# Gate and up of an FNet + GEGLU kernel: the last two contraction tiles taken into the seven Strassen products, and the columns run through in two passes with prepared weights fetched back

## The chip, the cores and the metric

One core of a Trainium2 chip runs the whole program. The metric is the device time of one execution in microseconds (us). Three executions of the kernel before took 781.22 (the median), 781.18 and 783.29 us. The engines are PE (matrix multiply; PEld is its weight load, which runs beside it), DVE (vector), ACT (scalar), POOL (GpSimd) and SP (here it only issues DMAs). Each engine takes its instructions in program order, and waits where one of them waits.

## The reference

```python
xn = _layernorm(x)                                     # x: 2048 x 448
a, b = xn @ dft_hid_re.T, xn @ dft_hid_im.T
s = dft_seq_re @ a - dft_seq_im @ b                    # 2048 x 2048 by 2048 x 448, twice
h = gelu_tanh(xn @ w_gate) * (xn @ w_up)               # 448 -> 1792
g = silu(h @ w_down)                                   # 1792 -> 448
out = x + s * g
```

Everything is float32. The kernel gets float32 accuracy out of PE by splitting each operand into a high part (a rounded copy, made by ACT) and a low part (the rest, a subtraction on DVE), and by multiplying high by high, high by low and low by high: three matmuls for one product.

## The kernel before

The 2048 rows lie in four chunks of 512 columns of the transposed activation (`xth[c]`, `xtl[c]`, high and low), and the 448 features lie in four contraction tiles of 128: tiles 0 to 2 are full, tile 3 has 64 features, with their low parts stacked under them, so that tile 3 needs two matmuls in place of three. The 1792 hidden columns are 14 blocks `f` of 128.

Four stages follow each other on PE. (1) Normalizing, transposing and plain gate and up products for blocks 0 and 1, up to 72 us. (2) Blocks 2 to 13, from 72 to 408 us, in 24 steps: a step is one block `f` with one pair `p` of chunks (2p and 2p+1), written in `strassen`, L372. (3) The transform along the hidden axis, `hid_mm`, to 489.5 us. (4) The transform along the sequence, to the end.

A step of stage 2 does gate and up of two chunks. Contraction tiles 0 and 1 go through Strassen's seven products with Winograd's sums: seven calls of `three` (L357) into four PSUM banks x1 to x4 (x1, x3 and x4 are used twice). Tiles 2 and 3 are added in plain products by `other` (L364), five matmuls for each of the four outputs; one of these, up of the second chunk, has a bank of its own, x5. A step has 41 matmuls of 512 columns. Between them stand up to four calls `dn[0]` to `dn[3]`, each of which takes one entry of the list `dq`: a down product of an earlier block pair, six matmuls of 448 columns (`down_one`), whose result DVE adds to `gacc` (L349). DVE takes the sums of the seven products from PSUM, ACT applies gelu, and the hidden values are split into high and low (`hs`). The last part of that for the second chunk is put off into the next step (`late`).

The sums of activations that Strassen needs, `t1` to `t4` of each pair (`combine`, L179), are made once, before and in the first steps. The sums of weights are made by `prep_s` (L238) for each block: four additions on POOL, copies on ACT, subtractions on DVE. Blocks go two at a time (`GROUPS`), and each block meets both pairs before the next two come: (0, f), (0, f+1), (1, f), (1, f+1), as (pair, block). So in each step either one block of weights or one pair of down weights (`prep_d`) is prepared, at the call `preps` in the middle of the step, and weights lie in three slots of `a_w`.

Beside this, stage 2 makes the sums of the sequence matrices that stage 4 needs (`sum_step`, L646): in every third step SP copies two halves of 896 KB from one DRAM tensor to another, and two steps later POOL issues two DMAs that add a second tensor to them. SP's DMAs land in the order of issue; POOL's run on a queue of their own.

Of the kernel before, what the change touches and what calls it, by code (L numbers as in the profile page):

```python
# [47 lines left out]
def fnet_geglu(ctx: ExitStack, tc: tile.TileContext, x, ca, ct, cp, et, wgu, wd, out):  # L48
# [29 lines left out]
    a_w = [a_ws[:, 2560 * i :][:, :2560] for i in (0, 2, 1)]  # L78
# [18 lines left out]
    th, tl = [None, None], [None, None]  # L97
# [71 lines left out]
    def turn_split(*turned):  # L169
        for c, k, pt in turned:  # L170
            nc.scalar.activation(xth[c][:, :, k * P : (k + 1) * P], pt, AF.Copy)
        for c, k, pt in turned:
            nc.scalar.activation(xf[c][:, :, k * P : (k + 1) * P], pt[:, :2], AF.Copy)
        for c, k, pt in turned:
            sl = slice(k * P, (k + 1) * P)
            nc.vector.tensor_sub(xtl[c][:, :, sl], pt, xth[c][:, :, sl])


    xf = [part(a_t, 1024 * (c + 1), 2, 512) for c in range(2)] + [None, None]  # L179

    def combine(p):


        (b11, b21), (b12, b22) = [[xf[c][:, k] for k in range(2)] for c in (2 * p, 2 * p + 1)]
# [4 lines left out]
        t = sb.tile([P, 2, 4, 512], FR, name=f"thl{p}", tag=f"u{p}")  # L189
        th[p], tl[p] = t[:, 0], t[:, 1]  # L190
        t = b11, b22, b12, b21

        def one(i):
            split(th[p][:, i], tl[p][:, i], t[i])

        return one


    loads = [0]

    def raw_tile():
        loads[0] += 1
        return a_r[:, 1536 * (loads[0] % 2) :][:, :1536]

    def load_w(f):
        raw = raw_tile()
        nc.sync.dma_start(raw[:, :1024], wgu[f].rearrange("p b f -> p (b f)"))
        return raw
# [34 lines left out]
    def prep_s(slot, raw, eng):  # L243


        w = a_w[slot]
        a21, a11, a12, a22 = [raw[:, i * P : (i + 1) * P] for i in range(2, 6)]
        s1, s2, s3, s4 = [raw[:, i * P : (i + 1) * P] for i in range(8, 12)]
        eng.tensor_add(s1, a21, a22)
        eng.tensor_sub(s3, a11, a21)  # L250
        eng.tensor_sub(s2, s1, a11)
        eng.tensor_sub(s4, a12, s2)
        nc.scalar.activation(w[:, :256], raw[:, :256], AF.Copy)
        nc.scalar.activation(w[:, 256:1408], raw[:, 384:], AF.Copy)
        nc.vector.tensor_sub(w[64:, :256], raw[64:, :256], w[64:, :256].bitcast(F32))
        nc.vector.tensor_sub(w[:, 1408:], raw[:, 384:], w[:, 256:1408].bitcast(F32))

        names = ("k3g", "k3u", "a11", "a12", "a22", "k2g", "k2u", "s1", "s2", "s3", "s4")
        parts = {}
        for i, n in enumerate(names):  # L260
            h = w[:, i * P : (i + 1) * P]
            l = w[:, 1408 + (i - 2) * P : 1408 + (i - 1) * P] if i >= 2 else None
            parts[n] = h, l
        return parts

    def load_d(grp):
        rv = raw_tile()[:, : 2 * D].rearrange("p (f d) -> p f d", f=2)
# [4 lines left out]

    def prep_d(grp, rv, late=False):
        w = a_d[grp[0] // 2 % 2].rearrange("p (a f d) -> p a f d", a=2, f=2)
# [89 lines left out]
    def other(ps, w, g, c, first=False):  # L364

        three(ps, w["k2" + "gu"[g]], (xth[c][:, 2], xtl[c][:, 2]), first)
        for xt in (xth[c], xtl[c]):
            nc.tensor.matmul(  # L368
                ps, w["k3" + "gu"[g]][0], xt[:, 3], start=False, stop=True, skip_group_check=True
            )  # L370

    def strassen(f, p, w, late, dn, preps):  # L372
# [5 lines left out]
        t1, t2, t3, t4 = [(th[p][:, i], tl[p][:, i]) for i in range(4)]  # L378
# [3 lines left out]

        x1 = bank(1)
# [9 lines left out]
        three(x3, w["s3"], t3, True)  # L393
        nc.vector.tensor_add(m, u, x3)
        x4 = bank(4)
        three(x4, w["s1"], t1, True)
        nc.vector.tensor_add(m, m, x4)
        three(x1, w["a12"], b21)
        other(x1, w, 0, c)
# [11 lines left out]
        other(x3, w, 1, c)  # L411
# [10 lines left out]
        other(x4, w, 0, e)  # L422
# [17 lines left out]
    with tc.manual_schedule():  # L440
# [109 lines left out]
        s_raw = load_w(GROUPS[1][0])  # L550
# [28 lines left out]
        xf[2] = part(a_t, 0, 2, 512)  # L579
# [18 lines left out]
        norm(1)  # L598

        nws = [None, None]  # L600


        for c in (2, 3):
            if c == 2:
                draw = load_d(GROUPS[1])
            else:
                s_raw2 = load_w(GROUPS[1][1])
            m0, h0, l0 = gateup(0, c, ws[0])
            between, between1 = [lambda: (m0(), h0()), l0], []
            if c == 2:  # L610

                xf[3] = part(a_g[1], 2560, 2, 512)
# [8 lines left out]
            else:  # L621
                between = [
                    lambda: (m0(), h0(), late_split(0)),
                    lambda: (l0(), late_split(1)),
                    lambda: late_split(2),
                    lambda: late_split(3),
                ]
            down(0, c - 1, wdn, between)
            if c == 2:
                nws[0] = prep_s(2, s_raw, nc.vector)  # L630
            else:
                nwdn, low_d = prep_d(GROUPS[1], draw, late=True)
                late_split = combine(1)
            m1, h1, l1 = gateup(1, c, ws[1], between1)
            m1()
            if c == 2:
                h1()
                l1()
                late_split = combine(0)
# [22 lines left out]

        dq = [(0, 3, wdn, kk) for kk in range(4)]
# [5 lines left out]
        nop = lambda: None  # L669

        slots = [2, 0, 1]
        e_at = {}
        for gi in range(1, len(GROUPS)):
            grp = GROUPS[gi]
            nxt = GROUPS[gi + 1] if gi + 1 < len(GROUPS) else None
            ws, wdn = nws, nwdn
            nws, n_raw = [None, None], {}

            def low_then_load():
                low_d()  # L680
                n_raw[0] = load_w(nxt[0])

            def prep_first():
                if gi == 1:
                    ws[1] = prep_s(slots[1], s_raw2, nc.vector)

            def prep_a():
                if gi == 1:
                    for n in range(4):
                        late_split(n)  # L690
                elif nxt:
                    nws[0] = prep_s(slots[2], n_raw[0], nc.gpsimd)
                else:
                    e_split(0)

            def prep_d_next():
                nonlocal nwdn
                if gi == 1:
                    nws[0] = prep_s(slots[2], n_raw[0], nc.gpsimd)
                    n_raw[1] = load_w(nxt[1])  # L700
                if nxt:
                    nwdn = prep_d(nxt, n_raw["d"])
                else:
                    e_split(1)
# [500 lines left out]
```

## Time and profile before

| what | us |
|---|---|
| median of three executions | 781.22 |
| profiled execution, whole | 780.67 |
| profiled execution, span from the first to the last instruction | 778.9 |
| stage 1, to the first product of `strassen` | 72.0 |
| stage 2, 24 steps | 336.5 |
| stage 3 | 81.1 |
| stage 4 | 289.4 |
| POOL's tensor instructions in stage 2, per 128 columns, alone | 0.46 |

Read the page from the engine that is busiest: its share of the span, then the chain that ended last, then what the other engines wait for. The mean duration of one matmul in the groups is longer than the distance between two, since matmuls overlap; the chain gives the distance.

### The profile page before, as it was taken

To read this page: it belongs to the slowest core of one execution; us is meant where nothing else is said; L and a number is where in the kernel's file an instruction comes from. 1 tells how busy PE (TensorE), PEld (TensorE's weight loads), DVE (VectorE), ACT (ScalarE), POOL (GpSimd) and SP (SyncE) were. 2 spreads that over 40 slices of the span, in tenths; PEclk is the share of its full clock that TensorE was granted. 3 is DMA by queue.
4 is the path that set the end of the run, shared out by engine and by line. 5 is a ranking of instruction groups with operands and counts; after the bars stand their busy time and mean duration, and the time that the engine had idled before them with its cause. 6 is when DMAs were issued, how large, how long until landed. Compare 5 with 4: busy or idle time off the path is not lost.

```text
span 778.9 us, 11227 instructions
## 1 busy us (share of the span) xinstructions
PE 772.5 (99%) x4092; PEld 695.8 (89%) x4092; DVE 594.5 (76%) x1052; ACT 310.5 (40%) x436; POOL 52.7 (7%) x83
## 2 busy tenths in 40 slices
PE   9999999999999999999999999999999999999997
PEld 8988888888888888888889999999999999999997
DVE  7877877767766776776675676888797887979797
ACT  3774432331332222322232855544444444444441
POOL 2000211110110010100000000000000000000000
PEclk9999999999999999999999999999999999999999
DMA  8000575353292360547000651688797969697884
GB/s 317 28 7 21 178 211 118 122 122 118 51 255 57 122 124 22 164 116 174 24 24 21 284 232 47 202 289 243 275 288 245 320 219 348 204 341 216 301 277 170
DMA packets 66103, 134.37 MB, mean 173 GB/s; under 512 B 6784, under 2 KB 53760, under 8 KB 65152
## 3 DMA queue, kind: packets, MB, share of 16 engines
q1 hardware_dynamic: 61008, 109.22, 40.4%
q0 software_dynamic: 4896, 24.32, 14.2%
q8 instruction: 32, 0.52, 0.3%
q14 instruction: 23, 0.19, 0.1%
q10 hardware_dynamic: 144, 0.11, 0.0%
HBM read 119.87 MB, written 43.12 MB: 209 GB/s over the span
## 4 chain that ended last, share of the span: by engine, by line
PE 97%; DVE 2%; issue 0%; ACT 0%; DVEq 0%
PE x L360 23%; PE p L1006 21%; PE po L340 17%; PE p L1009 10%; PE ab L824 9%; PE x L368 6%; PE gu L290 3%; PE py L1026 1%; PE py L1028 1%; PE py L1027 1%; PE gu L478 1%; PE warm L459 1%; PE pt L166 1%; DVE st L134 0%; DVE xr L157 0%
## 5 line engine op out<-in xcount | busy, mean ns | idle before, releaser
L340 PE MATMUL po<-wd,hs 128*128 128x448 f32 x672 | 153.0, 366 | 0.0
L340 PEld LDWEIGHTS po<-wd,hs 128*128 128x128 f32 x672 | 125.7, 188 | 14.4
L360 PE MATMUL x<-xt,w 128*128 128x512 f32 x504 | 135.0, 391 | 0.0
L360 PEld LDWEIGHTS x<-xt,w 128*128 128x128 f32 x504 | 94.6, 188 | 16.9
L349 DVE TENSOR_TENSOR gacc<-gacc,po 128x448 f32<-128x448 f32 x96 | 59.0, 617 | 60.3 <-PE po L340 60.3
L121 ACT ACTIVATE w<-raw 128x896 fp32r<-128x896 f32 (+1 forms) x60 | 54.6, 911 | 64.5 <-DVE raw L914 37.9
L360 PE MATMUL x<-thl,w 128*128 128x512 f32 x288 | 77.2, 391 | 0.0
L824 PE MATMUL ab<-w,xt 128*128 128x448 f32 x256 | 68.0, 365 | 0.0
L360 PEld LDWEIGHTS x<-thl,w 128*128 128x128 f32 x288 | 54.1, 188 | 10.9
L368 PE MATMUL x<-xt,w 128*128 128x512 f32 x192 | 59.2, 390 | 0.0
L1006 PE MATMUL p<-xt,w 128*128 128x448 f32 x168 | 54.3, 374 | 0.0
L415 ACT ACTIVATE hs<-tmp 128x512 fp32r<-128x512 f32 x24 | 15.2, 634 | 95.4 <-DVE tmp L413 95.4
L824 PEld LDWEIGHTS ab<-w,xt 128*128 128x128 f32 x256 | 48.1, 188 | 3.8
L400 ACT ACTIVATE tmp<-x 128x512 f32<-128x512 f32 x24 | 14.4, 598 | 89.1 <-PE x L368 89.1
L121 ACT ACTIVATE w<-f 128x896 fp32r<-128x896 f32 (+1 forms) x34 | 30.2, 889 | 40.8 <-DVE f L914 20.7
L122 DVE TENSOR_TENSOR w<-raw,w 128x896 fp32r<-128x896 f32 (+1 forms) x41 | 42.9, 1047 | 4.4 <-ACT w L121 2.9
L368 PEld LDWEIGHTS x<-xt,w 128*128 128x128 f32 x192 | 36.0, 188 | 7.7
L913 DVE TENSOR_TENSOR raw<-raw 128x128 f32<-128x128 f32 x69 | 19.8, 287 | 22.5 <-DMA raw<-sums 22.5
L1006 PE MATMUL p<-ts_u,ts_tmp 128*128 128x448 f32 x112 | 36.3, 374 | 0.0
L1006 PE MATMUL p<-ts_u,w 128*128 128x448 f32 x112 | 36.3, 374 | 0.0
L1006 PE MATMUL p<-hs,w 128*128 128x448 f32 x112 | 35.5, 374 | 0.0
L824 PE MATMUL ab<-wd,xt 128*128 128x448 f32 x96 | 35.1, 365 | 0.0
(250 smaller groups left out, 1605.0 us busy)
## 6 DMA issues: line engine op xcount, KB each, us to landing
ts_u<-td SPq DMA_DIRECT2D x48, 448.0 KB, 6.5
sums<-ca SPq DMA_DIRECT2D x16, 896.0 KB, 7.3
sums<-ca POOLq DMA_DIRECT2D x16, 896.0 KB, 9.0
raw<-ct SPq DMA_DIRECT2D x69, 192.0 KB, 4.0
raw<-sums SPq DMA_DIRECT2D x69, 128.0 KB, 4.4
f<-ct SPq DMA_DIRECT2D x39, 192.0 KB, 3.9
raw<-wgu SPq DMA_DIRECT2D x14, 512.0 KB, 3.7
td<-ts_u POOLq DMA_DIRECT2D x4, 1568.0 KB, 6.9
```

The source lines that it names most:

```text
L121: nc.scalar.activation(h, src, AF.Copy)
L122: nc.vector.tensor_sub(l, src, h)
L290: nc.tensor.matmul(ps[:, cols], a, xt[:, k, cols], start=n == 0, stop=n == len(mm) - 1)
L340: nc.tensor.matmul(po[:, :D], hs[:, a, kk * P : (kk + 1) * P], wdn[:, b, i], start=n == 0, stop=n == 5,)
L349: nc.vector.tensor_add(ga, ga, po[:, :D])
L360: nc.tensor.matmul(ps, a[i], b[j], start=first and n == 0, stop=n == 2, skip_group_check=True)
L368: nc.tensor.matmul(ps, w["k3" + "gu"[g]][0], xt[:, 3], start=False, stop=True, skip_group_check=True)
L415: nc.scalar.activation(hs[:, 0], g1, AF.Copy)
L824: nc.tensor.matmul(p[:, :D], a, b, start=n == 0, stop=n == len(mm) - 1)
L913: nc.vector.tensor_add(s2, cr1, s1)
L1006: nc.tensor.matmul(ps[q][:, :D], h, v, start=u % UN == 0, stop=False, skip_group_check=True)
L1009: nc.tensor.matmul(ps[q][:, :HD], l, v[:, :HD], start=False, stop=u % UN == NS - 1, skip_group_check=True,)
```

## The change

Contraction tiles 2 and 3 no longer go through `other`. For a pair whose sums are at hand (`q`), each of the seven products takes, into the same bank, a second product of weight sums and activation sums, over tile 2 or over a stack of tiles 2 and 3. Three matmuls are added to four of the products (`three`), two to the other three (`two`), and bank x5 falls away. Where the sums are not there yet (p = 0: blocks 2, 3, 4; p = 1: block 2), the step is as before.

The sums `t` and `q` of both pairs do not fit at once, so the steps now run over all blocks with pair 0, and then over all blocks with pair 1. Each step of the first pass prepares one block of weights (`weights`: five instructions on POOL over 960 columns in all, one copy of 1920 columns on ACT, subtractions of 1408 columns and of 512 columns by 64 rows on DVE) and stores it to DRAM; the second pass fetches prepared weights into three slots, one or two steps ahead. Down weights are stored and fetched likewise. Activations are written whole to DRAM (`whole`), from where the parts for the sums are read back; the accumulators `gacc` of chunks 2 and 3 are written out and read back, and `a_x[1]` too, whose place holds the sums `q` of pair 1.

```diff
+    def whole(c):
+        n = 1024 if c < 2 else 0
+        h, l = [a_x[c][:, 2048 * i + n : 2048 * (i + 1)].bitcast(F32) for i in range(2)]
+        nc.sync.dma_start(xw[c][:, n:], h)
+        nc.gpsimd.dma_start(xw[c][:, n:], l, accum_op=ALU.add)
...
+    def sums_s(eng):
+        r = raw_s.rearrange("p (b f) -> p b f", b=17)
+        eng.tensor_add(r[:, 1:16:14], r[:, 0:14:13], r[:, 8:17:8])
+        eng.tensor_sub(r[:, 3:15:11], r[:, 6:13:6], r[:, 0:14:13])
+        eng.tensor_sub(r[:, 2], r[:, 1], r[:, 6])
+        eng.tensor_sub(r[:64, 11], r[:64, 15], r[:64, 12])
+        eng.tensor_sub(r[:, 4:6], r[:, 7:10:2], r[:, 2:12:9])
+    def split_s(slot):
+        h, l = slot
+        src = raw_s[:, P:]
+        nc.scalar.activation(h, src[:, :WH], AF.Copy)
+        nc.vector.tensor_sub(l, src[:, :WL], h[:, :WL])
+        nc.vector.tensor_sub(h[64:, WL:], src[64:, WL:WH], h[64:, WL:].bitcast(F32))
+        return parts_of(slot)
...
+    def fetch_s(f, slot):
+        nc.sync.dma_start(slot[0].bitcast(F32), w_at[f][:, :WH])
+        nc.sync.dma_start(slot[1].bitcast(F32), w_at[f][:, WH:])
+        return parts_of(slot)
...
+        def weights(f):
+            if f < NF:
+                sums_s(nc.gpsimd)
+                w_of[0, f] = split_s(slots[f % 2])
+                if f + 1 < NF:
+                    load_s(f + 1)
+                else:
+                    t1_load()
+                store_s(f, slots[f % 2])
...
         x1 = bank(1)
         three(x1, w["a11"], b11, True)
+        if q:
+            two(x1, w["k3g"], k3)
...
         three(x2, w["s2"], t2, True)
+        if q:
+            three(x2, w["s2q"], q[2])
...
         three(x3, w["s3"], t3, True)
+        if q:
+            two(x3, w["s3q"], q[3])
...
         three(x1, w["a12"], b21)
-        other(x1, w, 0, c)
+        if q:
+            three(x1, w["k2g"], k2[0])
+        else:
+            other(x1, w, 0, c)
...
-        x5 = bank(5)
-        other(x5, w, 1, e, True)
-        nc.vector.tensor_add(m, m, x5)
+        if not q:
+            x5 = bank(5)
+            other(x5, w, 1, e, True)
+            nc.vector.tensor_add(m, m, x5)
...
+                elif f == 4:
+                    q = None
+                    prep = then(lambda: q_step(2), prep)
+                    dn[2] = then(send, lambda: q_step(3))
+                if f == NF - 1:
+                    fetch(2)
+                if f % 2 == 0 and f > 2:
+                    d_raw[0] = load_d(GROUPS[g])
+                elif f > 3:
+                    prep = then(prep, lambda: weights_d(g))
...
+                if f == NF - 1:
+                    q_load1(0)
+                    dn[1] = then(send, t1_sums)
+                    prep = then(prep, *[lambda i=i: t1_split(i) for i in (1, 2)])
+                    dn[2] = then(send, lambda: t1_split(3))
+                    dn[3] = then(send, lambda: t1_split(4))
+            else:
+                prep = nop
+                if f == 2:
+                    q = None
+                    q_load1(1)
+                    prep = lambda: (q_step1(0), q_step1(1))
+                    dn[2:] = then(send, lambda: q_step1(2)), then(send, lambda: q_step1(3))
+                    fetch(3)
...
+                if 3 <= f < NF - 2:
+                    fetch(f + 2)
```

Below, "step (0, 10)" is pair 0 with block 10. The first place is PE in step (0, 10), its first half, before and then now (`x_10_0` are the banks x1, x2, x3, x4 in turn, `thl` and `t` hold the sums of tiles 0 and 1, `tq` those of tiles 2 and 3, `po` is a down product):

```order
L360 MATMUL x_10_0_2369<-xt_66,w 128x512 x3
L360 MATMUL x_10_0_2376<-thl_680,w 128x512 x3
...
L360 MATMUL x_10_0_2390<-thl_680,w 128x512 x3
L360 MATMUL x_10_0_2395<-thl_680,w 128x512 x3
L360 MATMUL x_10_0_2369<-xt_66,w 128x512 x6
L368 MATMUL x_10_0_2369<-xt_66,w 128x512 x2
```

```order
L405 MATMUL x_10_0_1649<-xt_66,w 128x512 x3
L417 MATMUL x_10_0_1649<-xt_66,w 128x512 x2
L405 MATMUL x_10_0_1658<-t_742,w 128x512 x3
L405 MATMUL x_10_0_1658<-tq_801,w 128x512 x3
...
L405 MATMUL x_10_0_1675<-t_742,w 128x512 x3
L417 MATMUL x_10_0_1675<-tq_801,w 128x512 x2
L405 MATMUL x_10_0_1682<-t_742,w 128x512 x3
L417 MATMUL x_10_0_1682<-tq_801,w 128x512 x2
L405 MATMUL x_10_0_1649<-xt_66,w 128x512 x6
```

Each product has grown by two or three matmuls, the plain products have gone, and the whole step has 39 matmuls where it had 41.

The second place is DVE in step (0, 13), the last of the first pass, from its second down product on, now (L394 adds a down product, L214 to L217 are `combine` for pair 1, L321 the low part of down weights, L128 a low part of `t1`, L485 the low part of hidden values, L491 the last sum from bank x4):

```order
L394 TENSOR_TENSOR gacc_70<-gacc_70,po_1_1_2011 128x448
L214 TENSOR_TENSOR raw<-raw 128x512
L215 TENSOR_TENSOR raw<-raw 128x512
L216 TENSOR_TENSOR raw<-raw 128x512
L217 TENSOR_TENSOR raw<-raw 128x512
L321 TENSOR_TENSOR wd_73<-raw,wd_73 128x896
L128 TENSOR_TENSOR t_2023<-raw,t_2023 128x512 x2
L477 TENSOR_TENSOR tmp<-tmp,x_13_0_1990 128x512
L478 TENSOR_TENSOR tmp<-tmp 128x512
L394 TENSOR_TENSOR gacc_70<-gacc_70,po_1_2_2040 128x448
L128 TENSOR_TENSOR t_2023<-raw,t_2023 128x512
L485 TENSOR_TENSOR hs_76<-tmp,hs_76 128x512
```

Before, a step of block 11 had there:

```order
L349 TENSOR_TENSOR gacc_71<-gacc_71,po_3_1_2503 128x448
L255 TENSOR_TENSOR w<-raw,w 64x256
L256 TENSOR_TENSOR w<-raw,w 128x1152
L409 TENSOR_TENSOR tmp<-tmp,x_11_0_2519 128x512
L412 TENSOR_TENSOR tmp<-tmp,x_11_0_2484 128x512
L413 TENSOR_TENSOR tmp<-tmp 128x512
L349 TENSOR_TENSOR gacc_71<-gacc_71,po_3_2_2537 128x448
L420 TENSOR_TENSOR hs_76<-tmp,hs_76 128x512
```

Two instructions stood between the second down product and the sums of the step; seven stand there now, and an eighth ahead of L485.

The third place is SP's queue around the end of step (0, 11) and steps (0, 12) and (0, 13), now (`wss` is a raw block of weights, `wp` and `dp` are prepared weights in DRAM, `ca` the sequence matrices, `xw` whole activations):

```order
L265 DMA raw<-wss 128x1024
L266 DMA raw<-wss 128x2x128
L300 DMA wp_95<-w 128x1920
L301 DMA wp_95<-w 128x1408
L834 DMA dp_101<-wd_74 128x1792
L756 DMA sums_811<-ca 128x1792 x2
L310 DMA raw<-wd 128x2x448
L769 DMA raw<-xw_83 128x1024
L769 DMA raw<-xw_84 128x1024
L300 DMA wp_96<-w 128x1920
L301 DMA wp_96<-w 128x1408
L304 DMA w<-wp_85 128x1920
```

Before, SP's queue had in stage 2, for three to four steps:

```order
L207 DMA raw<-wgu 128x1024
L657 DMA sums_787<-ca 128x1792 x2
L207 DMA raw<-wgu 128x1024
L268 DMA raw<-wd 128x2x448
L207 DMA raw<-wgu 128x1024
```

The reads of raw weights and the copies of the sequence matrices stay; the stores of prepared weights come between them, and the first fetch of the second pass stands behind all of it.

More of the change, by code (lines that the diff above doesn't have):

```diff
@@ L47, in fnet_geglu @@
 @with_exitstack
-def fnet_geglu(ctx: ExitStack, tc: tile.TileContext, x, ca, ct, cp, et, wgu, wd, out):
+def fnet_geglu(ctx: ExitStack, tc: tile.TileContext, x, ca, ct, cp, et, wgu, wss, wd, out):
     nc = tc.nc
@@ L188, in combine @@
         nc.vector.tensor_sub(b21, b21, b22)
[L189 to L203, printed above, removed]
+        return {1: b11, 2: b22, 3: b12, 4: b21}
     def load_w(f):
-        raw = raw_tile()
-        nc.sync.dma_start(raw[:, :1024], wgu[f].rearrange("p b f -> p (b f)"))
+        raw = a_r[:, 1024 * f :][:, :1024]
+        nc.sync.dma_start(raw, wgu[f].rearrange("p b f -> p (b f)"))
         return raw
@@ L241, in block @@
         return wh[:, i * P : (i + 1) * P], wl[:, (i - 2) * P : (i - 1) * P]
[L243 to L263, printed above, removed]
-        return parts
+    raw_s = a_r[:, : 17 * P]
@@ L366, in other, with two, strassen @@
         three(ps, w["k2" + "gu"[g]], (xth[c][:, 2], xtl[c][:, 2]), first)
[L367 to L372, printed above, removed]
+        two(ps, w["k3" + "gu"[g]], (xth[c][:, 3], xtl[c][:, 3]))
+    def two(ps, a, b):
+        for x_ in b:
+            nc.tensor.matmul(ps, a[0], x_, start=False, stop=True, skip_group_check=True)
+    def strassen(f, p, w, q, late, dn, preps):
         c, e = 2 * p, 2 * p + 1
```

310 lines of the change are left out of this document (202 added, 108 removed).

## The prediction, made before the changed kernel was run

> **What bounds the kernel now.** The page comes first: busy shares, then the chain that ended last, then what PE waits for.
>
> ```profile
> span 778.9 us, 11227 instructions
> PE 772.5 (99%) x4092; PEld 695.8 (89%) x4092; DVE 594.5 (76%) x1052; ACT 310.5 (40%) x436; POOL 52.7 (7%) x83
> PE 97%; DVE 2%; issue 0%; ACT 0%; DVEq 0%
> PE warm L459 <- DVE hs L449: 1.5, 1, 1.5
> PE gu L478 <- DVE xt L176: 0.4, 1, 0.4
> ```
>
> PE is busy for 99% of the span and makes 97% of the chain. The two last rows are the whole answer on PE's waits (time, count, longest): 1.9 us, at the very start. So matmuls taken away shorten the kernel only while nothing else comes late, and any operand that comes late lengthens it by the full delay.
>
> What is one matmul worth? The chain in order of time, cut from one step, answers (start, length, piece), and the group row beside it answers otherwise:
>
> ```profile
> 103.63 1.36 PE x L360 x6
> 104.99 0.45 PE x L368 x2
> 105.44 1.21 PE po L340 x6
> ...
> 112.29 2.74 PE x L360 x12
> L360 PE MATMUL x<-xt,w 128*128 128x512 f32 x504 | 135.0, 391 | 0.0
> ```
>
> Twelve matmuls of 512 columns follow each other in 2.74 us: 0.2285 us each. The group's mean of 391 ns is how long one is under way; they overlap, and it would overstate the gain by 70%. A down product (six of 448 columns) takes 1.21 us. A step is 41 x 0.2285 + 4 x 1.21 = 14.2 us; with 39 matmuls it is 13.75.
>
> How much room has DVE, which feeds PE?
>
> ```profile
> L349 DVE TENSOR_TENSOR gacc<-gacc,po 128x448 f32<-128x448 f32 x96 | 59.0, 617 | 60.3 <-PE po L340 60.3
> L423 DVE TENSOR_TENSOR tmp<-tmp,x 128x512 f32<-128x512 f32 x24 | 16.5, 687 | 4.8 <-PE x L368 4.8
> L256 DVE TENSOR_TENSOR w<-raw,w 128x1152 fp32r<-128x1152 f32 x12 | 16.3, 1359 | 1.7 <-ACT w L254 1.4
> L276 DVE TENSOR_TENSOR wd<-raw,wd 128x896 fp32r<-128x896 f32 x7 | 7.6, 1084 | 0.0
> L122 DVE TENSOR_TENSOR thl<-tmp,thl 128x512 fp32r<-128x512 f32 x6 | 4.4, 733 | 2.7 <-ACT thl L121 2.6
> 203.00:217.00 14.00, 14.00 (x65) 12.02 (x65) 10.52 (x17) 3.94 (x6) 3.38 (x6) 1.00 0.51 111
> ```
>
> The last row is a stretch of 14 us, about one step (busy time of PE, PEld, DVE, ACT and POOL, then granted clock, DMA share, GB/s): DVE works 10.5 of 14 us. By the other rows a step's standing work on DVE is ten instructions at 0.69 and four at 0.62, 9.4 us.
>
> **The change part by part.** *Matmuls.* A step with sums has 39 matmuls where it had 41: 9 steps of pair 0 and 11 of pair 1, so 40 x 0.2285 = **-9.1 us**. This assumes that the new matmuls, of the same shape, follow each other as the old ones do. The down products and stages 3 and 4 keep theirs.
>
> *Steady steps.* Each step of pass 1 prepares a whole block. By columns, DVE's 1359 ns for 1152 and 687 for 512 give 1.63 for 1408; the stack at 64 rows has 512 columns, 0.69. ACT's copy of 1920 columns follows from these rows:
>
> ```profile
> L254 ACT ACTIVATE w<-raw 128x1152 fp32r<-128x1152 f32 x12 | 13.9, 1156 | 1.4 <-DVE raw L252 1.4
> L121 ACT ACTIVATE thl<-tmp 128x512 fp32r<-128x512 f32 x6 | 3.7, 624 | 0.0
> L400 ACT ACTIVATE tmp<-x 128x512 f32<-128x512 f32 x24 | 14.4, 598 | 89.1 <-PE x L368 89.1
> L252 POOL TENSOR_TENSOR raw<-raw 128x128 f32<-128x128 f32 x10 | 5.8, 576 | 0.8
> raw<-wgu SPq DMA_DIRECT2D x14, 512.0 KB, 3.7
> ```
>
> It takes 1.8 us. DVE loses one addition (x5): 9 x 0.69 + 2.5 + 2.3 = 11.0 of 13.75 us, so it keeps up. In time: bank x1 is complete after 27 matmuls and one down product, 7.4 us into the step; gelu 0.6, copy 1.8, low parts 2.3 put the next block's weights at about 12.2 of 13.75 us. The raw block, issued there, lands some 3.7 us later (the like did), 2.2 us into the next step; POOL's 960 columns take 4.3 us at 0.58 for 128, to 6.5, and the next copy wants them at 8. It fits by 1.5 us: **0**. If the load lands late the cover is gone; that is a rival.
>
> *The start.* Step (0,4) prepares a block and makes two sums `q`. A sum costs a subtraction 0.69, ACT's copy 0.62 and a low part 0.73, about 2.0 with waiting for ACT. DVE: 9.4 + 2.3 + 4.0 + 1.2 waiting for the long copy = 16.9 against 14.2, 2.7 over; step (0,3), with one sum, just fits. The weights of block 5 and `q[3]`, `q[4]` are used early in (0,5). Bounds: +1 if the lag is taken by DVE's idle time, +5 if the reloads for the sums come late too. I take **+3.5**, the overrun plus some waiting for reloads.
>
> *The pair boundary on DVE.* Step (0,13) has nine instructions at 0.69, four at 0.62, four of `combine`, down weights 1.08, four low parts at 0.73 and about 1.3 of waiting for ACT: 16.7 us, 3.0 over. Step (1,2) has 9.4 plus four sums, 17.4 us, 3.2 over. Together 6.2 late. Step (1,3) needs `q[3]` only after 14 matmuls and a down product, 4.4 us in; DVE needs 2.65 after the last down product for it (0.62 + 2.0), which leaves 1.75. So 4.4 are lost at least, plus small waits on the way: **+5** (4 to 5.5).
>
> *The first fetch.* Block 2's weights come back behind SP's queue (third place above): 1024 KB of activations, 1664 stored, 1664 fetched, 4352 KB. Speed of the queues, from the table of DMA issues (KB, us to landing) and from windows:
>
> ```profile
> raw<-wd SPq DMA_DIRECT2D x1, 448.0 KB, 3.0
> ...
> raw<-wd SPq DMA_DIRECT2D x1, 448.0 KB, 11.0
> sums<-ca SPq DMA_DIRECT2D x16, 896.0 KB, 7.3
> sums<-ca POOLq DMA_DIRECT2D x16, 896.0 KB, 9.0
> 117.16 1.67 POOL L659 DMA_DIRECT2D sums<-ca  x2
> 119.23 0.38 SPq L268 DMA_DIRECT2D raw<-wd  x1
> 123.00:125.00 2.00, 2.00 (x11) 1.73 (x10) 1.48 (x3) 0.97 (x2) 0.00 (x0) 1.00 0.99 226
> 440.00:444.00 4.00, 4.00 (x22) 3.70 (x21) 2.97 (x6) 3.67 (x5) 0.00 (x0) 1.00 0.96 394
> ```
>
> The same load of down weights lands after 3.0 us alone (issued at 176.2) and after 11.0 when issued at 119.23, 2 us behind POOL's pair of adding copies. While those run the engines are 99% busy at 226 GB/s; plain transfers make 394, about 400 KB a us, and 3.0 us for 448 KB leaves 1.9 fixed. So 4352 KB take 10.9 + 1.9 = 12.8 us. The queue starts at 12.2 in (0,12), and PE wants block 2 after 1.55 + 13.75 = 15.3 us: it fits. But in pass 2 POOL has no weights to sum, at the end of pass 1 it is free early, and its two halves of 896 KB at 220 take 8.1 us of the engines: 20.9, or 5.6 late. Bounds 0 and 4.5, since part lies beside the boundary's stall on DVE; I take **+3**.
>
> *Block 4's fetch*, wanted two steps (28.0 us) later, stands behind 768 KB of reads, block 3's 1664, the accumulators' 1792, down weights 896, a copy of 1792 and its own 1664: 8576 KB, 23.3 us; with a pair of adding copies 31.4. Allowing for the boundary's stalls, 0 to 4.2: **+2.5**. From block 6 on a fetch has two whole steps: 0.
>
> *Elsewhere.* Stage 1 trades one `combine` and split for another and adds writes of activations; stages 3 and 4 keep their order: 0, within 1.
>
> Sum: -9.1 + 3.5 + 5 + 3 + 2.5 = +4.9. The profiled execution took 780.67 us, so it would take 785.6; the median lies 0.55 above that execution, which is small beside the terms, so I leave the sum there.
>
> **The rivals.** *A, the gain is seen.* The transfers land in time and DVE's lags are mostly taken up: the start costs 1, the boundary 3 to 5. 780.7 - 9.1 + 4 to 6 = 775.6 to 777.6. For it: the DMA share of many slices of stage 2 is low, and DVE idles 3 us a step. Against it: the counted overruns have no idle time within their own steps. *B, a draw.* DVE's lags cost in full (8.5), transfers fit: 780.1. For it: 12.8 is under 15.3, so only the adding copies stand against the fetch. *C, much slower.* Adding copies delay the raw loads of pass 1 as well:
>
> ```profile
> DMA  8000575353292360547000651688797969697884
> ```
>
> Of the slices of stage 2 (the 5th to 21st figure) eight stand at 3 or less: they have room now. The new stores fill them: a pass-1 step reads 640 KB of raw weights (512 before) and stores 1664 KB, with a third of a round of copies beside. Where a raw load takes 11.0 us in place of 3.7, weights come about 3.7 us late; twice makes 7.4, so 793, from the point where a load lands over 1.5 us late. That no matmul is saved at all is not open: the order shows 39 in a step. That the new ones are slower is possible if each weight tile is changed for one matmul only; as in the rows above, every matmul has its load already (x4092 both), at 89% of the span. I give that no chance of its own.
>
> A stall can cost more than its length if the clock falls. Here every window reads 1.00, PE's longest wait is 1.5 us, and the opening shows the price:
>
> ```profile
> 1.49 5.92 PE warm L459 x14
> ```
>
> These 14 took 0.423 each, 0.19 above the later ones. The Trainium skill, "TensorE: Matmul & The Clock Gate", section "What's actually happening", says that PE's clock is halved after an idle window of about 3.4 us and needs as long a busy stretch to return; no row here shows a stall so long. By that rule, as an estimate, a stall of that length would cost about 1.6 us more.
>
> By the row alone: if a late fetch stops PE for longer than any wait here, and the next 8 to 16 matmuls run at 0.423, that is 1.6 to 3.1 us on top, and lies inside C.
>
> **How the numbers follow.** A 0.25, B 0.23, forecast (784 to 789) 0.40, C 0.12. About 0.3%, 2.34 us, can be told from no change: under 778.9 is faster, over 783.6 slower, against 781.22. So faster 0.25, same 0.23, slower 0.52. Range 776.0 to 792.5: it reaches into A and takes in the upper bounds of the terms; half of C and a tail of A stay out. Of the sign "slower" alone, 784 to 792.5.
>
> **What would show it.** Right: PE has 4052 matmuls, steady steps take 13.75 us without waits, and PE's waits sum to some 14 us in four places: (0,4) to (0,5) and (1,2) to (1,3) for DVE (`tq`, `hs`, weights), the start of (1,2) and of (1,4) for a DMA into `w`. Wrong: no DMA wait at (1,2) (then B or A); waits in (0,6) to (0,12) (then C); steady steps above 13.8 (then the products are dearer); a granted clock under 1.00 after a stall. What I trust least is the adding copies' place beside the first fetch: moved by one step, 5.5 us go.

## The result, and the profile after it

Four executions of the changed kernel took 804.55, 805.49, 807.24 and 809.79 us: a median of 806.37 against 781.2 before, a ratio of 1.0321 (95% interval 1.0281 to 1.0362). It is slower by 25 us. The forecast was slower, 785.6, with 792.5 as the upper end of the range: the direction was right, and the size missed by 21 us. The profiled execution is the fastest of the four, 804.55, with a span of 802.8. (One of the ten executions of the version at the end of "Moving the adding copies" took 1532.24 us beside nine at 781.89 to 783.76; nothing in the runs explains it, and that version's ratio leaves it out.)

First the page of the changed kernel: busy shares, DMA share of the engines by slices, the chain by engine, and four rows from the table of DMA issues (KB each, us from issue to landing).

```profile
span 802.8 us, 11336 instructions
PE 774.4 (96%) x4052; PEld 691.3 (86%) x4052; DVE 598.2 (75%) x1045; ACT 316.2 (39%) x424; POOL 76.0 (9%) x102
DMA  8476894999979999858852281396978979696985
PE 79%; DMA 8%; DVE 6%; ACT 3%; POOL 2%; issue 2%; SPq 0%; DVEq 0%; POOLq 0%; ACTq 0%
sums<-ca SPq DMA_DIRECT2D x16, 896.0 KB, 11.0
sums<-ca POOLq DMA_DIRECT2D x16, 896.0 KB, 11.4
wp<-w SPq DMA_DIRECT2D x12, 960.0 KB, 7.3
w<-wp SPq DMA_DIRECT2D x12, 960.0 KB, 9.5
```

PE's 4052 matmuls are 40 fewer, as the change says. The chain no longer lies on PE alone: 8% of it is DMA, and six of the nine full slices of the first pass (the 5th to 13th figure) stand at 9, where before only one slice of stage 2 did. What PE waited for (time, count, longest):

```profile
PE x L405 <- DMA w<-wp: 8.5, 2, 8.1
PE x L405 <- DVE tmp L491: 7.1, 1, 7.1
PE x L405 <- DVE w L291: 1.5, 2, 0.9
PE po L385 <- ACT gacc L392: 1.4, 2, 1.0
PE x L405 <- ACT tmp L360: 1.0, 1, 1.0
PE x L405 <- ACT w L290: 0.7, 1, 0.7
```

The first is a DMA by name. The second names DVE, but DVE had waited itself. Step (0,5) shows how such a wait is followed back, over PE, DVE, POOL and SP in the timeline (start, length, instruction, and in brackets the idle time before it and what ended it):

```profile
116.55 1.37 PE L385 MATMUL po<-wd,hs 128*128 128x448 f32 x6
124.98 1.65 PE L405 MATMUL x<-t,w 128*128 128x512 f32 x3 [7.06 <-DVE tmp L491]
...
114.94 0.61 DVE L394 TENSOR_TENSOR gacc<-gacc,po 128x448 f32<-128x448 f32 x1
121.12 0.69 DVE L692 TENSOR_TENSOR tmp<-tmp 128x512 f32<-128x512 f32 x1 [5.57 <-DMA tmp<-xw]
124.26 0.67 DVE L491 TENSOR_TENSOR tmp<-tmp,x 128x512 f32<-128x512 f32 x1
...
105.96 1.70 POOL L758 DMA_DIRECT2D sums<-ca  x2
108.26 0.32 SPq L681 DMA_DIRECT2D tmp<-xw  x1
109.65 1.13 SPq L683 DMA_DIRECT2D tmp<-xw  x2
```

PE waits for a bank that L491 frees; L491 stands on DVE behind L692, a subtraction for the sums `q` (`q_step(3)`); L692 waits for the activations read back by SP, issued at 108.3 and 109.7; and POOL had issued its pair of adding copies at 106.0. No engine lacks time here: DVE and PE both stand still for reads of 512 KB in all.

The waits for weights L290 and L291 are a second place of the same kind: the raw load of block 12, issued at 207.3 behind adding copies of 202.9, and the first matmuls of (0,12), which wanted its result (the load's row: KB, us to landing):

```profile
raw<-wss SPq DMA_DIRECT2D x1, 512.0 KB, 10.7
202.92 1.66 POOL L758 DMA_DIRECT2D sums<-ca  x2
...
223.33 0.73 PE L405 MATMUL x<-xt,w 128*128 128x512 f32 x2 [0.69 <-ACT w L290]
224.99 0.50 PE L405 MATMUL x<-xt,w 128*128 128x512 f32 x1 [0.93 <-DVE w L291]
```

Where the time went, step by step. A step starts with its first matmul into x1 on PE's timeline; what it should take is 39 or 41 matmuls at 0.2285 us and its down products at 1.21.

| place | should take | took | lost |
|---|---|---|---|
| (0,2) to (0,4), from 72.19 | 37.8 | 41.8 | 4.0 |
| (0,5) | 13.8 | 23.4 | 9.7 |
| (0,6) to (0,8) | 41.3 | 41.3 | 0 |
| (0,9) to (0,12) | 55.0 | 61.7 | 6.7 |
| (0,13) to (1,3) | 41.7 | 53.7 | 11.9 |
| (1,4) to the end of stage 2, 431.85 | 137.6 | 137.7 | 0.1 |
| stage 2 | 327.4 | 359.7 | 32.3 |

Before, stage 2 took 336.5. The steps that nothing delays took 13.77 us each, where the steps before took 14.23; so the saving of 9.1 us over the 20 shorter steps is there in full, and 32.3 us of lateness lie over it. Stages 3 and 4 are as before within 0.4 us.

### The profile page after: what moved, and what is told of

Same layout as the page of the kernel before. It is cut to its first block, busy times and chain, and to the rows that moved or that the text cites. A ratio compares the mean times of both kernels' runs of the same rounds, so it can differ in the third digit from the quotient of the medians.

```text
span 802.8 us, 11336 instructions
## 1 busy us (share of the span) xinstructions
PE 774.4 (96%) x4052; PEld 691.3 (86%) x4052; DVE 598.2 (75%) x1045; ACT 316.2 (39%) x424; POOL 76.0 (9%) x102
## 4 chain that ended last, share of the span: by engine, by line
PE 79%; DMA 8%; DVE 6%; ACT 3%; POOL 2%; issue 2%; SPq 0%; DVEq 0%; POOLq 0%; ACTq 0%
PE p L1175 20%; PE x L405 16%; PE po L385 13%; PE p L1178 10%; PE ab L991 9%; PE x L417 3%; DMA w<-wp 3%; PE gu L335 2%; DMA raw<-wss 2%; PE py L1195 1%; PE py L1197 1%; PE py L1196 1%; DMA tmp<-xw 1%; ACT w L290 1%; PE gu L546 1%
## 5 line engine op out<-in xcount | busy, mean ns | idle before, releaser
L405 PE MATMUL x<-xt,w 128*128 128x512 f32 x450 | 121.5, 395 | 10.7 <-DMA w<-wp 8.5
L405 PEld LDWEIGHTS x<-xt,w 128*128 128x128 f32 x450 | 85.0, 189 | 28.9 <-issue 8.4
L405 PE MATMUL x<-t,w 128*128 128x512 f32 x276 | 83.4, 404 | 8.3 <-DVE tmp L491 7.1
L394 DVE TENSOR_TENSOR gacc<-gacc,po 128x448 f32<-128x448 f32 x96 | 58.7, 616 | 36.0 <-PE po L385 35.8
L405 PEld LDWEIGHTS x<-t,w 128*128 128x128 f32 x276 | 53.1, 194 | 19.6 <-DVE tmp L491 7.9
L127 ACT ACTIVATE w<-f 128x896 fp32r<-128x896 f32 (+1 forms) x34 | 30.2, 889 | 42.7 <-DVE f L1081 18.9
L128 DVE TENSOR_TENSOR w<-raw,w 128x896 fp32r<-128x896 f32 (+1 forms) x41 | 42.8, 1047 | 4.3 <-ACT w L127 3.8
L1220 POOL DMA_DIRECT2D cc<-x x14 | 12.4, 882 | 289.3 <-DVE raw L1080 107.4
L417 PE MATMUL x<-xt,w 128*128 128x512 f32 x116 | 37.0, 399 | 1.1 <-ACT xt L127 0.5
L1175 PE MATMUL p<-ts_g,w 128*128 128x448 f32 x112 | 36.4, 374 | 0.0
## 6 DMA issues: line engine op xcount, KB each, us to landing
sums<-ca POOLq DMA_DIRECT2D x16, 896.0 KB, 11.4
```

The lines of the kernel that those rows point to most:

```text
L127: nc.scalar.activation(h, src, AF.Copy)
L128: nc.vector.tensor_sub(l, src, h)
L394: nc.vector.tensor_add(ga, ga, po[:, :D])
L405: nc.tensor.matmul(ps, a[i], b[j], start=first and n == 0, stop=n == 2, skip_group_check=True)
L417: nc.tensor.matmul(ps, a[0], x_, start=False, stop=True, skip_group_check=True)
L1175: nc.tensor.matmul(ps[q][:, :D], h, v, start=u % UN == 0, stop=False, skip_group_check=True)
```

## The experiments

Theory 1: POOL's adding copies for the sums of the sequence matrices hold the DMA engines just when SP's loads are wanted, and the changed kernel wants many loads soon after their issue. Theory 2: it is the volume of SP's own queue, the new stores above all. Theory 3: DVE and ACT have too much to do at the start and at the pair boundary.

### Without the adding copies, in both kernels

```diff
                     if d == 0:
                         nc.sync.dma_start(a, b)
-                    else:
-                        nc.gpsimd.dma_start(a, b, accum_op=ALU.add)
```

> The kernel before, with the eight pairs of adding copies into the sums of the sequence matrices left out (so those sums are incomplete). Theory 1 (adding copies beside SP's loads make them land late, and the changed kernel has no cover for it): in the kernel before nothing waits for a DMA in stage 2, so the adding copies cost nothing there: 781, within 1 us. Theory 2 (the sheer volume of SP's queue, the stores above all): also 781. A control: if it falls by more than 2 us, the adding copies already cost time before, and neither theory is complete.

> The changed kernel with the same eight pairs of adding copies left out (sums incomplete). Theory 1: the waits for reloads at the start of (0,5), for weights in (0,9) to (0,12) and for the first fetch go; what is left is DVE's overrun, about 3.5 at the start and 5 at the pair boundary: 806.4 - 10 - 6.6 - 7 = about 783. Theory 2: stores and fetches stay, so do the waits: over 800. Theory 3 (DVE and ACT have too much work at the start and the boundary, and the DMA waits only lie beside it): over 800 too.

The kernel before took 781.52 (ratio 1.0007, 0.9997 to 1.0016): adding copies cost it nothing. The changed kernel took 782.32 (1.0011, 1.0001 to 1.0021), 24 us less than with them, and stage 2 took 337.1 in place of 359.7. The same reads of `tmp` at 108 to 110 us, first in the changed kernel, then without adding copies (KB, us to landing):

```profile
tmp<-xw SPq DMA_DIRECT2D x1, 256.0 KB, 10.0
tmp<-xw SPq DMA_DIRECT2D x2, 128.0 KB, 10.9
```

```profile
tmp<-xw SPq DMA_DIRECT2D x1, 256.0 KB, 2.9
tmp<-xw SPq DMA_DIRECT2D x2, 128.0 KB, 3.0
```

Ten against three us for the same read. The raw load of block 12, which took 10.7 us above, shows it too, here without adding copies:

```profile
raw<-wss SPq DMA_DIRECT2D x1, 512.0 KB, 3.4
```

That is Theory 1; what is left over the 327.4 us, 9.7 us, is the most that Theory 3 can have (0.9 of it is still a wait for the first fetch).

### Only the first pair left out

```diff
-                if (at - d) % 3 or not 0 <= j < NK // 2:
+                if (at - d) % 3 or not 0 <= j < NK // 2 or (d and j == 0):
```

> The changed kernel with only the first pair of adding copies (issued in (0,4)) left out, so one sum is incomplete. Theory 1: the wait of 7.1 us in (0,5) and the slow clock behind it go, 8 to 9 us, and all later waits stay: 797 to 799. If the reloads for the sums q are late by SP's own queue: within 2 us of 806.

One execution: 796.98. In (0,5) the wait of 7.06 has become 0.88, and the step takes 14.9 us in place of 23.4. The later waits are all there, the one for the fetch with 8.39 where it had 8.06; those for weights have grown, and the steps (0,8) to (0,12) lose 8.7 us where they lost 6.7.

```profile
255.43 1.19 PE L405 MATMUL x<-xt,w 128*128 128x512 f32 x2 [8.39 <-DMA w<-wp]
```

One pair of adding copies, in one step, costs 8.5 us in (0,5).

### Without the stores

```diff
             def weights(f):
-                store_s(f, slots[f % 2])
...
             def fetch_s(f, slot):
-        nc.sync.dma_start(slot[0].bitcast(F32), w_at[f][:, :WH])
-        nc.sync.dma_start(slot[1].bitcast(F32), w_at[f][:, WH:])
+        nc.sync.dma_start(slot[0].bitcast(F32), w_at[2][:, :WH])
+        nc.sync.dma_start(slot[1].bitcast(F32), w_at[2][:, WH:])
```

> The changed kernel without the stores of the prepared weights of blocks 3 to 13 (11 x 1664 KB less written); each fetch reads block 2's weights in place of its own, so the second pass computes with wrong weights. Adding copies stay. Theory 1: the first fetch comes 4.2 us earlier, the waits at (0,5) and in (0,9) to (0,12) stay almost whole: 799 to 803. Theory 2: all these waits go: about 783. Theory 3: 804 to 807.

802.28 (ratio 1.0251, 1.0209 to 1.0293), with executions from 795.86 to 803.63. The median lies where Theory 1 put it, but the trace, of the fastest of them, says more than that. PE's waits in (0,5) and for the first fetch:

```profile
124.13 1.65 PE L405 MATMUL x<-t,w 128*128 128x512 f32 x3 [6.65 <-DVE tmp L491]
248.46 0.70 PE L405 MATMUL x<-xt,w 128*128 128x512 f32 x2 [0.34 <-DMA w<-wp]
250.13 0.50 PE L405 MATMUL x<-xt,w 128*128 128x512 f32 x1 [0.97 <-DMA w<-wp]
```

The wait in (0,5) stays; those for weights in (0,9) to (0,12), which I had expected to stay, are gone in this execution, and PE waits 1.3 for the first fetch in place of 8.5. So (0,5) is the adding copies' alone, while the later waits needed adding copies and stores together here: without either of the two they go. The other three executions took 5.7 to 7.8 us longer than this one and have no trace, so whether their weights came in time is not known; how much of the later waits is the stores' stays open.

### Is it the addition, or a second queue?

```diff
-                        nc.gpsimd.dma_start(a, b, accum_op=ALU.add)
+                        nc.gpsimd.dma_start(a, b)
```

> The changed kernel with POOL's copies at their old places but without the addition: plain copies of the same 896 KB (the sums lack the first addend). Theory 1a (the addition makes them slow, as it reads both tensors: 226 GB/s beside 394): they hold the engines for about 4.5 us in place of 8, so loads land about 3.5 us earlier; three long waits shrink by about half: 806.4 - 10 to 14 = 792 to 796. Theory 1b (any second queue beside SP's, or the bytes written, is what counts): within 4 us of 806.

792.94 (ratio 1.0143, 1.0128 to 1.0158), 13 us less. POOL's copies land in 7.3 us (median) where the adding ones took 11.4, the two long waits shrink by a third, and those for weights in (0,9) to (0,12) are gone:

```profile
sums<-ca POOLq DMA_DIRECT2D x16, 896.0 KB, 7.3
121.72 1.65 PE L405 MATMUL x<-t,w 128*128 128x512 f32 x3 [4.32 <-DVE tmp L491]
250.09 1.19 PE L405 MATMUL x<-xt,w 128*128 128x512 f32 x2 [5.36 <-DMA w<-wp]
```

About half of the 24 us go with the addition, the other half with 1792 KB more beside the loads even as plain copies. An adding copy also reads a second tensor; whether it is slower for that, or for the adding itself, no run separates.

### Moving the adding copies: four tries

First the adding copies alone were written later: four pairs after steps (1,6) to (1,12), four in stage 3.

```diff
-            for d in (0, 2):
...
+            if at % 3 == 0:
+                sum_copy(at // 3, 0)
+            if at in ADD_AT:
+                sum_copy(ADD_AT.index(at), 2)
+        ADD_AT = 16, 18, 20, 22
...
+            if k in (3, 5, 7, 9):
+                sum_copy((k + 5) // 2, 2)
```

> The changed kernel with the adding copies moved out of the first pass: four pairs in every second step of the second pass from (1,6) on, four between the blocks of stage 3. Theory 1: as without them, about 783, within 2 us, since in the second pass a fetch has two whole steps. Theory 2 and theory 3: over 800.

827.4 (ratio 1.0592, 1.0576 to 1.0608): 44 us over the expectation, and 21 over the changed kernel. POOL's issues, PE's wait for the first fetch, and PE's longest wait in stage 4 show why:

```profile
218.51 2.54 POOL L763 DMA_DIRECT2D sums<-ca  x3
231.56 0.84 POOL L763 DMA_DIRECT2D sums<-ca  x1 [10.52 <-issue]
...
253.97 0.83 POOL L763 DMA_DIRECT2D sums<-ca  x1 [5.07 <-issue]
271.55 1.19 PE L405 MATMUL x<-xt,w 128*128 128x512 f32 x2 [32.47 <-DMA w<-wp]
PE p L1182 <- DVE xt L128: 11.1, 1, 11.1
```

The eight adding copies written for (1,6) and later were issued from 218.5 to 254 us, in the last two steps of the first pass: nothing on POOL stands between them and the last block's weight sums, and their copies had long landed. They met the fetch that PE wanted first. Of the four pairs of stage 3, the last adding copies landed at 530.8 us, when stage 4 had begun (523.7), and stage 4 took 13.8 us longer than in the changed kernel.

Next, copy and adding copies of a pair stand together, so that POOL waits for SP and SP for PE: five pairs in the second pass, three in stage 3.

```diff
-            for d in (0, 2):
...
+            if at in (14, 16, 18, 20, 22):
+                sum_copy(at // 2 - 7, 0)
+                sum_copy(at // 2 - 7, 2)
...
+            if k in (3, 6, 9):
+                sum_copy(k // 3 + 4, 0)
+            if k in (5, 8, 11):
+                sum_copy((k + 1) // 3 + 3, 2)
```

> The changed kernel with copy and adding copies of a pair of sequence matrices together, out of the first pass: five pairs in steps (1,4) to (1,12), every second one, three between the blocks of stage 3. In the run before, the adding copies had been given a later place in program order only; POOL had nothing to wait for and ran all of them at once, at 238 to 270 us. Here each waits for its copy on SP's queue, which waits for PE to free a slot of weights, so it cannot run ahead. Theory 1: 783, within 2 us (782.3 without any adding copies). Theory 2 (volume of SP's queue) and theory 3 (DVE): over 795, since all stores, fetches and DVE work stay.

800.38 (ratio 1.0247, 1.0224 to 1.027). Stage 2 took 337.4, as without adding copies; the loss has moved to the end of stage 3 and the start of stage 4 (18 us more than in the changed kernel), where the last pairs still ran, SP's copies in the queue ahead of the loads wanted there and POOL's adding copies beside them:

```profile
477.40 0.81 POOL L760 DMA_DIRECT2D sums<-ca  x1 [6.97 <-DMA sums<-ca]
493.18 0.81 POOL L760 DMA_DIRECT2D sums<-ca  x1 [14.97 <-DMA sums<-ca]
...
507.98 0.74 PE L1181 MATMUL p<-ts_u,ts_tmp 128*128 128x448 f32 x1 [9.72 <-DVE xt L128]
```

Then three pairs as halves in the first pass, one half a step, the other five in the second pass as above.

```diff
+                h = at - 2 - d
+                if 0 <= h < 6:
+                    sum_copy(h // 2, d, halves[h % 2 :][:1])
...
```

> The changed kernel with three pairs of copies and adding copies cut into halves of 896 KB, one adding half a step in (0,6) to (0,11), issued when POOL has made the step's sums (about 6.5 us into it; 4 us long, so done before the next raw load is issued at 12.2); the other five pairs in (1,4) to (1,12). Theory 1: the first pass and the boundary as without adding copies, and nothing left for stage 3: 782, within 2 us. If an adding copy costs by being there at all in the first pass, and not by standing beside a load that is wanted soon: over 788.

792.25 (ratio 1.0132, 1.0115 to 1.0149), 10 us over the expectation; most of it is one wait, for the weights of (0,10), and the slow clock behind it:

```profile
167.18 0.81 POOL L764 DMA_DIRECT2D sums<-ca  x1
184.83 0.72 POOL L281 TENSOR_TENSOR raw<-raw 128x256 f32<-128x256 f32 x1 [16.85 <-DMA raw<-wss]
189.75 1.22 PE L405 MATMUL x<-xt,w 128*128 128x512 f32 x2 [4.86 <-ACT w L290]
```

SP had a store of 2 MB (`sp<-xt`, issued at 162.2) in its queue, the raw load behind it was issued at 171.5, and POOL could begin its sums only at 184.8, 13.3 us after the issue, where in the steps around it they began 5.7 to 8.6 us after. Two halves of 896 KB stood beside that store, SP's own plain one (issued at 159.6, ahead of it in the same queue) and POOL's adding one (167.2); which of the two cost more is not separated.

Last, all eight pairs behind (1,3), one of them in stage 3.

```diff
-            for d in (0, 2):
...
+            steps = 14, 16, 18, 20, 21, 22, 23
+            if at in steps:
+                sum_copy(steps.index(at), 0)
+                sum_copy(steps.index(at), 2)
...
+            if k in (3, 4):
+                sum_copy(7, 2 * k - 6)
```

> The changed kernel with every copy and adding copy after step (1,3): seven pairs behind steps (1,4), (1,6), (1,8), (1,10) to (1,13), one in stage 3 (copy at its fourth block, addition at its fifth). In the run with halves the first pass still lost 9.5 us in (0,10), where a half stood beside a raw load behind the 2 MB store of activations; in the run with three pairs in stage 3 stage 4 lost 15 us, as the last two pairs were still adding at 470 to 500 us. Theory 1: neither is left; 782, within 2 us, as without adding copies, and the boundary and the start keep their 10 us of DVE's and ACT's lateness. If volume, not the place beside a wanted load, is what costs: over 788.

782.2 (ratio 1.001, 1.0 to 1.002), as expected, with stage 2 at 337.5, and with all the copies, stores and fetches that the changed kernel has. The same volume, then, cost nothing in these places; what cost was the place beside a load wanted soon. (SP's own copies of the sequence matrices have moved too; but with these at their old places and only the adding copies gone, the time was 782.32.)

### What is left: DVE at the start and at the boundary

In that version the waits of PE in stage 2 name ACT and DVE, and hardly a DMA. The largest:

```profile
PE po L385 <- ACT gacc L392: 1.4, 2, 0.9
PE po L385 <- DVE hs L485: 1.2, 1, 1.2
PE x L405 <- DVE tmp L491: 0.9, 1, 0.9
PE x L405 <- ACT tmp L360: 0.8, 1, 0.8
...
PE x L405 <- DMA w<-wp: 0.3, 1, 0.3
```

Steps (1,2) and (1,3) took 32.9 us (239.16 to 272.02) where 28.0 would do: 4.9 lost; the start loses another 5.2. Three kernels tried to take this back. One, on top of the version with three pairs in stage 3, spreads the sums `q` over one more step in each pass:

```diff
-                    dn[2] = then(send, lambda: q_step(3))
+                if f == 5:
+                    q = None
+                    dn[2] = then(send, lambda: q_step(3))
...
-                    dn[2:] = then(send, lambda: q_step1(2)), then(send, lambda: q_step1(3))
...
+                elif f == 3:
+                    q = None
+                    prep = lambda: q_step1(2)
+                    dn[2] = then(send, lambda: q_step1(3))
```

> As e4_sums_second_pass, and the sums q of tiles 2 and 3 are made over one more step in each pass: the fourth of pair 0 in (0,5), the third and fourth of pair 1 in (1,3); these two steps use the plain products, which costs 4 matmuls, 0.9 us. Theory 3 in its small form (DVE's overrun at (0,4) and (1,2) is what is left of the loss, about 1.2 + 1.9 us in the run without adding copies): 2 us under e4, about 780. If those waits have another cause: 1 us over e4.

800.45, against 800.38 of its base, and stage 2 took 337.5 against 337.4. It neither gained 2 us nor lost 1: the 0.9 us of matmuls was paid, and about as much was got back, 1.7 us less lost at the boundary and 0.8 more at the start. (The executions of either kernel spread over 2.5 to 3.1 us, so it is stage 2 of the two traces that says this, not the medians.) One, on top of the version with halves, makes `t1`'s four sums one down product earlier:

```diff
-                    dn[1] = then(send, t1_sums)
+                    dn[0] = then(send, t1_sums)
```

> As e7_halves_between, and the four sums of t1 in (0,13) stand behind the first down product in place of the second, where DVE is idle for 1.9 us (waiting for PE) in the runs above. If the boundary's remaining 5 us are DVE's overrun in (0,13) and (1,2): 1 to 2 us under e7. If they are not: the same as e7, or longer, where DVE then waits there for the activations' reload.

794.48, 2.2 us over its base. Here a weight block was late too (DVE waited 2.17 us for it in (0,13)), so it decides nothing on the boundary. The last, on top of the last version, moves work:

```diff
-                    dn[1] = then(send, t1_sums)
+                    t1_sums()
...
-                nc.vector.tensor_sub(b11, b12, b11)
+                nc.gpsimd.tensor_sub(b11, b12, b11)
```

The same replacement is made in the other subtractions of `q_step1` and, for pair 1, of `combine`.

> As e10_all_after_first_pass, and the eight subtractions at the pair boundary (four for t1 in (0,13), four for q in (1,2)) run on POOL, which has nothing to do there, in place of DVE. This takes 8 x 0.69 = 5.5 us off DVE, of the 6.2 by which its work in these two steps is over PE's. Theory 3 in its small form (the 5 us left at the boundary are DVE's overrun): about 4 us under e10, 778 to 779, and so under the kernel before. If they are ACT's, or the fetch's: within 1 us of e10, 782.

780.1 (ratio 0.9983, 0.9973 to 0.9993), 2.1 us under its base, half of what was expected, and by 0.17% under the kernel before. Steps (1,2) and (1,3) took 30.2 us (238.55 to 268.77), so 2.2 are lost in place of 4.9. The waits left there:

```profile
242.21 0.48 PE L385 MATMUL po<-wd,hs 128*128 128x448 f32 x1 [1.10 <-DVE hs L485]
244.48 1.65 PE L405 MATMUL x<-xt,w 128*128 128x512 f32 x6 [0.42 <-ACT tmp L437]
```

So DVE's overrun is the larger part of the boundary's loss, 2.7 us of 4.9; the rest was not taken apart further. At the start, the waits on PE in the version with all copies behind (1,3) name ACT for 2.2 us (in (0,2) to (0,4)) and DVE for 0.9 (in (0,5)); no run takes ACT's work away there.

## Why the prediction was wrong, point by point

- **Matmuls, -9.1 us: right.** Steps without a wait take 13.77 us, 39 matmuls at the distance read from the chain, 0.46 less than before, which is 9.2 in twenty steps. The mean of the group, 391 ns, would have promised 15.6.
- **The start, +3.5: this failed, and most of all.** It cost 13.7 in steps (0,2) to (0,5). I counted DVE's overrun and gave the reloads a share "if they come late too", with +5 as the end. DVE's and ACT's part was 5.2, as the version with all copies behind (1,3) shows, and it was not DVE's overrun in (0,4) as I had it: 2.8 of it was lost in (0,2) and (0,3) already, where I had counted nothing and where PE waits for ACT. The reloads' part was the other 8.5 (what leaving out the first pair took off (0,5)), since their landing was taken without asking what POOL issues just before. I had the rows for it: 448 KB landing after 11.0 us behind an adding copy and after 3.0 without. They went into the fetch term and rival C only. The first adding copies come in (0,4), 2 us ahead of the reload, and the order of the two queues could have told that.
- **Steady steps, 0: this failed too.** 6.7 us were lost in (0,9) to (0,12), where two raw loads lay beside adding copies and landed after 9.0 and 10.7 us in place of 3.7. The mechanism is that of rival C, priced at 7.4 us and given 0.12. The rival was right; it belonged in the sum, since adding copies run in every third step of the first pass whatever else is true, and the fit of 1.5 us could not hold a delay of 5 to 7.
- **The boundary: right in size by luck, wrong in how the parts add.** Predicted 5 for DVE, 3 for the first fetch, 2.5 for block 4's fetch, 10.5 in all; measured 11.9. DVE and small waits on ACT make 4.9 to 5.2 in the versions without the late fetch. The fetch had landed whole 25.8 us after the first of the 4352 KB was issued (20.9 predicted), and 17.7 without adding copies (12.8 predicted). Two things had been left out. The queue was not empty: 4.3 to 4.5 us passed until SP's load before them had landed. And without adding copies the 4352 KB then took 13.4 us, about 325 KB a us, not 400. PE waited 8.06 for the first part of the fetch, and part of DVE's lateness lay under that wait. Block 4's fetch cost nothing. The errors of the three terms happened to cancel.
- **The clock: right.** In the two long waits it fell to half, as the prediction had it. In (0,5) ten matmuls took 4.4 us in place of 2.3, so 2.1 on top, inside the 1.6 to 3.1.
- **The range.** Its upper end, 792.5, held the upper bounds of the terms (+10.1, 790.8) or rival C (793), not C on top of them; and even both, 798, would not have reached 806, since the start's bound of +5 was too low by 8.7. The late loads have one cause, which acts at three places at once: the bounds of such terms add, and -9.1 + 13.7 + 6.7 + 11.9 is +23.2, against +23.9 between the profiled executions.

Rival B, DVE's lags in full and all transfers in time, at 780.1, is close to what the changed kernel does without the adding copies (782.3) or with them in better places (782.2).

## What to carry to other kernels

When a change adds loads that are wanted soon after they are issued, list every transfer of the other queues with its time of issue, and price each load by the row that shows it beside such a transfer, at every place where the two meet; these delays have one cause and come together. A transfer on an idle engine's queue runs when its data is there, not where it is written (in the first try above, at 218.5 us, for a step that began at 332): it needs something to wait for that is itself paced by the work. And an engine waiting in order for a late read holds back all that stands behind it, so that the name in PE's list of waits may be that of an engine with nothing to do.

## What the runs showed of the hardware

Adding copies from DRAM to DRAM take longer than plain ones: POOL's 896 KB landed after 11.4 us (median) with the addition and 7.3 without, in the same kernel at the same places. Reads of 256 KB on SP's queue took 10.0 us beside them and 2.9 without.

PE's clock fell 5.3 us after each of the two long stops began (at 117.9 and 254.4 us), and stayed at half for 6.8 us. Three windows of the changed kernel, two from the first stop on and one from a third fall (the third figure from the right is the clock; a mean of 0.80 over 122 to 124 us says that it fell at 123.2):

```profile
122.00:124.00 2.00, 0.00 (x0) 0.00 (x0) 1.49 (x2) 0.48 (x1) 1.23 (x2) 0.80 1.02 428
124.00:130.00 6.00, 5.02 (x12) 3.97 (x13) 4.91 (x9) 1.75 (x3) 2.83 (x4) 0.50 0.26 103
225.00:226.00 1.00, 0.78 (x2) 0.47 (x3) 0.97 (x2) 0.00 (x0) 0.00 (x0) 0.79 0.00 0
```

It fell as well without one long stop: between 222.6 and 225.7 us PE had three waits of 0.2 to 0.9 us, with single matmuls among them, and the clock was at half from 225.6 to 229.0. The three falls of this trace (123.2, 225.6 and 259.7 us) and the three returns (130.0, 229.0 and 266.6) lie on one grid of 3.41 us: 30 steps of it between the first two falls, 10 between the last two. In each long stop, the clock fell at the end of the first step of that grid without any matmul (119.8 to 123.2 and 256.3 to 259.7). In the step before the third fall PE stood still for only 1.7 of 3.4 us; yet some 1.9 us of standing still, in the steps in which the two long stops began, did not make it fall. What decides between these stays open.

The Trainium skill, "TensorE: Matmul & The Clock Gate", section "What's actually happening", puts the limit at an idle window of about 3.4 us. The two long stops agree with it; the third case goes beyond it, since no wait there was longer than 0.93 us.
